# Down stage of a transformer block kernel: operands fetched ahead into idle buffers, fill work finished earlier, products reordered, last product split by bank

## The chip, the cores and the metric

One core of one Trainium2 chip. The metric is the device time of one execution in microseconds (us). A profile is of one execution and gives its span, from the first to the last instruction, which is some 2 us shorter than the device time. The engines are TensorE (PE in the profile; PEld is its weight load), VectorE (DVE), ScalarE (ACT) and SyncE, whose queue (SPq) issues nearly all transfers. PSUM is the memory that TensorE writes its results to; a tile in it is an accumulator, and a bank is a part of it. To evict an accumulator is to read its result out on another engine; a snap is such a read that adds an earlier sum, so that TensorE may go on in the same accumulator.

## The reference

The reference is one transformer block on 2048 tokens of width 1024: a linear-attention half, then a gated MLP half.

```python
h  = x + A_ref(layernorm(x), wqkv, wo)          # attention half, not touched by the change
# MLP half, on layernorm(h)
gate = x @ W_gate; up = x @ W_up                # 1024 -> 3584
hh   = relu(gate) * up
h2   = h + hh @ W_down                          # 3584 -> 1024
```

The change is about the last line, the down projection, and about what is done for it during gate and up.

## The kernel before

Every large product is computed with Winograd's form of Strassen's scheme: seven block products instead of eight, paid for with sums of blocks on VectorE. In the down stage this is done twice. There are seven *outer* products, of half-size blocks. Products 1 and 7 are then plain matmuls; products 2, 6, 5, 3 and 4 are again split into seven *inner* products, m1 to m7. Outer operand sums are made during the gate/up stage and stored to DRAM; inner operand sums are made on VectorE (t1 to t4 from W_down, s1 to s4 from x) while the outer product ahead is running.

During gate/up the sums of W_down are spread over the windows as *fill* work. There is one buffer, `wraw`, for the raw chunk:

```python
def wd_sums(c):
    def load():   # spool: raw = tile(tag="wraw", bufs=1); two dma_start of 512 KB
    def one():    # t1 = b12 - b11 on VectorE, first reader of raw
    ...           # two, three; four also stores the sums to DRAM
    return [load, one, two, three, four]

# per window (12 us of TensorE), how many fill items:
want = len(fill) // (nwin - k) if nwin - k > 1 else len(fill)
want = min(len(fill), max(want, 0))
```

An outer product that is split into inner ones, with its in-order instruction streams (the order in the program is the order on TensorE and on VectorE):

```python
cur["m1"]()                      # TensorE -> PSUM accumulator A
if prv: prv["11"](); pop()       # pop(): one operand sum of the NEXT product, on VectorE
cur["s1"]()                      # VectorE: snap = A + base
cur["m2"]()
if prv: prv["m4"]()              # rest of the previous product
cur["00"](); pop()               # eviction of an output block
if prv: prv["10"](); prv["m3"]()
late_w()                         # request W of the next product, queue its eight sums
pop()
cur["m6"]()                      # needs s2, t2
if prv: prv["01"]()
pop()
cur["m5"]()                      # needs s1, t1
cur["s2"]()                      # VectorE: second snap of A
pop(2)
cur["m7"]()                      # may overwrite A only after the second snap
```

Its x operand tiles and W tiles come from rotating pools that are opened after the gate/up pools are closed. (cut: attention half, gate/up products, launch; in the block above, the other loads and the third snap)

Of the kernel before, what the change touches and what calls it, by code (L numbers as in the profile page):

```python
# [31 lines left out]
def block_kernel(ctx: ExitStack, tc: tile.TileContext, x, wqkv, wo, wg, wu, wd, out, H: int):  # L32
# [417 lines left out]

    new_hn(0)
    wpool = mctx.enter_context(tc.tile_pool(name="wpool", bufs=2))
# [3 lines left out]
    def load_group(g):  # L456

        tiles, loads = [], []
        for nm, v in (("wg", wg_v), ("wu", wu_v)):
            w_sb = wpool.tile([P, KC, 2, GP * P], BF16, tag=nm, name=nm)  # L460
# [143 lines left out]
    def wd_sums(c):  # L604
# [4 lines left out]
        def load():  # L609
            st["raw"] = raw = spool[0].tile([P, 2, 2, D], BF16, tag="wraw", bufs=1, name="wraw")  # L610
            for k in range(2):
                nc.sync.dma_start(out=raw[:, k], in_=wd_k[:, k, 2 * c:2 * c + 2, :])
            st["b"] = [[raw[:, k, :, j * DW:(j + 1) * DW] for j in range(2)] for k in range(2)]

        def one():
            st["t"] = spool[0].tile([P, 4, 2, DW], FP16, tag="wt", bufs=1, name="wt")
# [104 lines left out]
    prepool = ctx.enter_context(tc.tile_pool(name="prepool", side="right", **reuse))  # L721
# [61 lines left out]

    runs = [(early[f // GP], f, f % GP, [1]) for f in range(NE)]
# [25 lines left out]
    for r, (wt, f, fi, toks) in enumerate(runs):  # L810
        w = [ops() for _, ops in now]
        later = []
        for n, s in enumerate(toks):
# [8 lines left out]
            if r >= NE:  # L822
                want = len(fill) // (nwin - k) if nwin - k > 1 else len(fill)
                want = min(len(fill), max(want, 0))
# [41 lines left out]
            if k == nwin - 1:  # L866
                b11 = [prepool.tile([P, FQ, DW], BF16, tag="b11", name="b11")]
                nc.sync.dma_start(out=b11[0][:], in_=wd_v[:, 0:FQ, 0:DW])
    assert not fill

    HW = DW // 2
    raws = {1: (0, 0), 2: (1, 0), 3: (1, 1)}
    sums_of = {4: 3, 5: 0, 6: 1, 7: 2}
    xslot = {2: H12, 3: S4, 4: H22, 5: S1, 6: S2, 7: S3}
    OUTER = (1, 2, 6, 5, 7, 3, 4)
    INNER = (2, 6, 5, 3, 4)
    outs = {2: (0, 0), 7: (1, 1), 3: (0, 1), 4: (1, 0)}
    full = slice(0, DW)
    ALL = slice(0, NT)

    def plain_mm(ps, x, w, p, kh):
        s, t0 = divmod(2 * p, NT)
        for t in range(2):
            for f in range(FQ):
                nc.tensor.matmul(ps[:, t * NW:(t + 1) * NW], lhsT=x[s][kh][:, f, (t0 + t) * P:(t0 + t + 1) * P],  # L885
                                 rhs=w[kh][:, f, :], start=(kh == 0 and f == 0),
                                 stop=(kh == 1 and f == FQ - 1), skip_group_check=True)

    first_ps = [acc("A")]
    wfirst = [b11[0][:], None]  # L890
    xfirst = [[t[:] for t in row] for row in x1]
    plain_mm(first_ps[0], xfirst, wfirst, 0, 0)
# [13 lines left out]
    def load_half(op, x):  # L906

        k = op["k"]
        w = dpool.tile([P, FQ, DW], BF16, tag="w", bufs=4, name="w")
        if k in raws:  # L910
            i, j = raws[k]
            nc.sync.dma_start(out=w[:], in_=wd_v[:, i * FH + x * FQ:i * FH + (x + 1) * FQ, j * DW:(j + 1) * DW])
        else:
            nc.sync.dma_start(out=w[:].bitcast(FP16), in_=t_dram[sums_of[k]][:, x * FQ:(x + 1) * FQ, :])
        op["wt"][x] = w
        op["w"][x] = w[:] if k in raws else w[:].bitcast(FP16)

    def load_x(op, s, kh):

        k = op["k"]  # L920
        t = (x1pool if op["n"] % 2 == 0 else dpool).tile([P, FQ, SW], BF16, tag="x", bufs=4, name="x")
        nc.sync.dma_start(out=t[:], in_=x_dram[s][kh][:, xslot[k], :, :])
        op["xt"][s][kh] = t
        op["x"][s][kh] = t[:].bitcast(FP16) if k in (3, 5, 6, 7) else t[:]

    def new_op(n):
        return {"n": n, "k": OUTER[n], "wt": [None] * 2, "w": [None] * 2,
                "xt": [[None] * 2 for _ in range(2)], "x": [[None] * 2 for _ in range(2)], "s": {}, "t": {}}
# [157 lines left out]
    for p in range(4):  # L1086
        plain_mm(pss[p], op["x"], op["w"], p, 1)
        sink1(p, pss[p])
        if p >= 1:
            pop(2)  # L1090
# [138 lines left out]
```

## Time and profile before

The median is 764.73 us (three runs, 763.38 to 764.73).

| what | before |
|---|---|
| span | 761.0 us |
| TensorE busy | 721.2 us, 95% |
| TensorE idle or at half clock in the down stage | 11.6 us |
| after the last matmul | 5.4 us |

The page of the kernel before, busy time per engine:

```profile
PE 721.2 (95%) x3951; PEld 381.3 (50%) x4004; DVE 565.7 (74%) x1022; ACT 326.5 (43%) x597; POOL 6.1 (1%) x44
```

The timeline of TensorE before, down stage, only the rows with an idle time. Columns: start us, length us, engine, source line, operation, out<-in, form, number of instructions, and in brackets the idle time before and who ended it.

```profile
602.48 6.20 PE L885 MATMUL accA<-w,x 128*128 128x512 bf16 x28 [3.03 <-DMA w<-in_B_W_down_dram]
...
615.00 3.23 PE L1042 MATMUL accA<-w,x 128*128 128x256 bf16 x28 [0.27 <-DMA x<-x_dram]
...
625.12 4.56 PE L1042 MATMUL accA<-ws,xs 128*128 128x256 f16 x28 [3.83 <-DVE snap L1048]
...
654.33 6.27 PE L1042 MATMUL accA<-w,x 128*128 128x256 f16 x56 [0.20 <-DVE snap L1048]
...
713.38 3.22 PE L1042 MATMUL accY<-w,x 128*128 128x256 bf16 x28 [1.09 <-DMA out_dram<-o]
...
717.40 3.22 PE L1042 MATMUL accA<-ws,xs 128*128 128x256 f16 x28 [0.80 <-DVE snap L1048]
...
724.17 6.27 PE L1042 MATMUL accA<-w,x 128*128 128x256 f16 x56 [0.51 <-DVE snap L1048]
...
752.37 3.22 PE L1042 MATMUL accX<-w,xs 128*128 128x256 f16 x28 [0.52 <-DVE o L1007]
```

Idle before these rows sums to 10.25 us. The row at 625.12 also takes 4.56 us for 28 matmuls where the other rows of 28 of this size take 3.22. The windows view of the kernel before shows why. Columns: window, its length, busy time (and instructions) of PE, PEld, DVE, ACT, POOL, granted TensorE clock, mean busy share of the 16 DMA engines (it can pass 1), GB/s.

```profile
621.00:624.00 3.00, 0.29 (x3) 0.10 (x2) 3.00 (x3) 0.00 (x0) 0.00 (x0) 1.00 1.02 421
625.00:627.00 2.00, 1.88 (x10) 1.28 (x10) 1.88 (x3) 0.00 (x0) 0.00 (x0) 0.50 0.97 401
628.00:630.00 2.00, 2.00 (x21) 1.80 (x19) 1.18 (x2) 0.00 (x0) 0.00 (x0) 1.00 0.98 401
```

In the middle row the clock is 0.50: TensorE runs at half speed after the idle time. In the first row VectorE is busy all the time (3.00 of 3.00 us): it makes the sums that it could not begin earlier. The last two columns show that the DMA engines were full meanwhile (401 to 421 GB/s). What VectorE had waited for in the same stage (view of waits, columns: total, times, longest):

```profile
DVE ws L960 <- DMA w<-in_B_W_down_dram: 11.1, 1, 11.1
DVE xs L973 <- DMA x<-x_dram: 7.4, 3, 6.0
```

It could not make product 2's inner sums until W_down and x had come, and TensorE then waited for VectorE.

### The profile page before, as it was taken

Reading aid. Unit: us, or ns where it says so; the run is one execution under the profiler, and the core shown is the slowest. Engines: PE = TensorE matmul, PEld = TensorE weight load, DVE = VectorE, ACT = ScalarE, POOL = GpSimd, SP = SyncE. Lnnn points to the kernel's source line nnn. Section 1 sums busy time; section 2 is a strip of 40 time slices with the busy share of each in tenths; the row PEclk is TensorE's granted clock in tenths of the full one; section 3 lists DMA queues with packets and bytes.
Section 4 is the critical chain, followed back from the end, with each engine's and each line's share of the span. In section 5 each row is a group of like instructions: output and inputs, shape, how many; then the busy total and the mean of one; then the engine's idle time right before and its main releaser. Section 6 shows DMA issues by size and latency. Waiting matters only on the chain.

```text
span 761.0 us, 10554 instructions
## 1 busy us (share of the span) xinstructions
PE 721.2 (95%) x3951; PEld 381.3 (50%) x4004; DVE 565.7 (74%) x1022; ACT 326.5 (43%) x597; POOL 6.1 (1%) x44
## 2 busy tenths in 40 slices
PE   5999999999889989999999999999999879999996
PEld 2443555444344434444444444444444358875685
DVE  5997654787896767687777877788776279947995
ACT  4876553878768554444444444444434010000000
POOL 0000000000000000000000000000000000000000
PEclk9999999999999999999999999999999999999999
DMA  9665002079767544166438356495543899967713
GB/s 318 153 138 152 1 1 107 5 165 224 193 160 183 121 118 145 42 180 185 147 105 246 102 157 221 165 279 178 177 172 122 292 405 333 362 236 255 266 29 97
DMA packets 146419, 132.03 MB, mean 173 GB/s; under 512 B 50880, under 2 KB 127936, under 8 KB 146368
## 3 DMA queue, kind: packets, MB, share of 16 engines
q1 hardware_dynamic: 138928, 127.16, 55.3%
q10 hardware_dynamic: 7440, 4.20, 1.9%
q8 instruction: 31, 0.51, 0.3%
q14 instruction: 20, 0.16, 0.1%
HBM read 79.95 MB, written 39.85 MB: 157 GB/s over the span
## 4 chain that ended last, share of the span: by engine, by line
PE 65%; DVE 16%; DMA 9%; ACT 5%; issue 2%; SPq 1%; POOL 0%; DVEq 0%; ACTq 0%
PE accA L753 22%; PE accX L753 8%; PE accY L753 8%; DMA x<-x_dram 5%; PE accA L1042 4%; PE attn L517 4%; PE Aq L285 3%; PE Aq L419 2%; PE Eq L285 2%; PE Aq L673 2%; PE accX L1042 2%; PE accY L1042 2%; DVE stats L254 2%; DVE o L1007 1%; DMA hn<-hn 1%
## 5 line engine op out<-in xcount | busy, mean ns | idle before, releaser
L763 ACT ACTIVATE gu<-gu 128x512 bf16<-128x512 bf16 x72 | 45.4, 631 | 122.3 <-DVE gu L762 122.3
L758 ACT COPY snap<-accA 128x1024 f32<-128x1024 f32 x72 | 72.7, 1010 | 44.9 <-PE accA L753 44.8
L517 PE MATMUL attn<-wo_mem,oT 128*128 128x512 bf16 x247 | 57.3, 379 | 4.1 <-DVE o_sb L497 3.4
L753 PEld LDWEIGHTS <-tg 128*128 128x128 f16 x384 | 37.6, 98 | 45.3
L753 PEld LDWEIGHTS <-tu 128*128 128x128 f16 x384 | 37.6, 98 | 45.3
L1042 PEld LDWEIGHTS <-x 128*128 128x128 f16 (+1 forms) x560 | 54.6, 98 | 9.9 <-DMA out_dram<-o 1.3
L152 ACT COPY u<-Aq 128x512 f32<-128x512 f32 x56 | 32.2, 581 | 44.9 <-PE Aq L285 21.3
L762 DVE TENSOR_TENSOR gu<-accY,snap 128x1024 bf16<-128x1024 f32 x36 | 43.9, 1220 | 10.2 <-ACT snap L758 10.2
L753 PE MATMUL accA<-hn,tg 128*128 128x512 f16 (+1 forms) x192 | 49.3, 379 | 0.0
L753 PE MATMUL accA<-hn,tu 128*128 128x512 f16 (+1 forms) x192 | 49.3, 379 | 0.0
L762 DVE TENSOR_TENSOR gu<-accX,snap 128x1024 bf16<-128x1024 f32 x36 | 43.9, 1220 | 7.0 <-ACT snap L758 3.9
L1042 PEld LDWEIGHTS <-xs 128*128 128x128 f16 x420 | 41.7, 99 | 11.1 <-issue 5.7
L753 PEld LDWEIGHTS <-wg 128*128 128x128 bf16 x288 | 28.2, 98 | 34.0
L753 PEld LDWEIGHTS <-wu 128*128 128x128 bf16 x288 | 28.2, 98 | 34.0
L517 PEld LDWEIGHTS <-oT 128*128 128x128 bf16 x256 | 24.9, 97 | 34.9 <-issue 6.7
L885 PEld LDWEIGHTS <-x 128*128 128x128 bf16 (+1 forms) x224 | 21.9, 98 | 29.2 <-issue 3.3
L1042 PE MATMUL accA<-w,x 128*128 128x256 f16 (+1 forms) x280 | 31.7, 273 | 1.0 <-DVE snap L1048 0.7
L766 DVE TENSOR_TENSOR hq<-gu 128x512 bf16<-128x512 bf16 x48 | 20.3, 423 | 14.9 <-ACT gu L763 14.9
L285 PEld LDWEIGHTS <-xT 128*128 128x128 bf16 (+1 forms) x192 | 18.6, 98 | 24.9 <-issue 3.4
L497 DVE TENSOR_TENSOR o_sb<-nd,rd 128x384 bf16<-128x384 f32 (+1 forms) x48 | 22.8, 507 | 8.6 <-ACT rd L496 8.3
L1048 DVE TENSOR_TENSOR snap<-accA,u 128x1024 f32<-128x1024 f32 x16 | 19.4, 1219 | 11.5 <-PE accA L1042 11.5
L519 DVE SCALAR_TENSOR_TENSOR x_res<-attn,x_res 128x512 bf16<-128x512 f32 x32 | 22.0, 688 | 6.3 <-PE attn L517 6.2
(199 smaller groups left out, 1368.4 us busy)
## 6 DMA issues: line engine op xcount, KB each, us to landing
x<-x_dram SPq DMA_DIRECT2D x24, 896.0 KB, 7.2
x_dram<-hq SPq DMA_DIRECT2D x28, 512.0 KB, 3.1
wg<-in_B_W_gate_dram SPq DMA_DIRECT2D x14, 512.0 KB, 5.0
wu<-in_B_W_up_dram SPq DMA_DIRECT2D x14, 512.0 KB, 7.2
wraw<-in_B_W_down_dram SPq DMA_DIRECT2D x14, 512.0 KB, 4.9
x_dram<-hq SPq DMA_DIRECT2D x28, 256.0 KB, 3.0
t_dram<-wt SPq DMA_DIRECT2D x28, 256.0 KB, 2.2
w<-t_dram SPq DMA_DIRECT2D x8, 896.0 KB, 8.4
```

Source lines behind the costliest of these rows:

```text
L152: nc.scalar.copy(out=snaps[nm, v], in_=A[v][:])
L285: nc.tensor.matmul(ps[:], lhsT=left[m - 1][:, kc, r + v * P:r + (v + 1) * P], rhs=right[m - 1][:, kc, :], start=(start and kc == 0), stop= ...
L497: nc.vector.tensor_tensor(out=ov[:, c0:c0 + n], in0=ndv[:, :, 0:P].rearrange("p k (h e) -> p k h e", h=HPC), in1=rd[:, 0:n, :].unsqueeze(3 ...
L517: nc.tensor.matmul(ps[:], lhsT=st["oT"][:, c, :], rhs=wo_sb[:, c, j * NW:(j + 1) * NW], start=(c == 0), stop=(c == KC - 1))
L519: nc.vector.scalar_tensor_tensor(out=h_sb[:, j * NW:(j + 1) * NW], in0=ps[:], scalar=1.0, in1=h_sb[:, j * NW:(j + 1) * NW], op0=ALU.mult, ...
L753: nc.tensor.matmul(ps[:, v, :], lhsT=w[v][n - 1][:, kc, :], rhs=left[n - 1][:, kc, :], start=(t is not None and kc == 0), stop=(kc == KH - ...
L758: nc.scalar.copy(out=st[nm][:], in_=halves(st["A"]))
L762: add(out=g[:], in0=halves(st[nm]), in1=st[base][:], op=ALU.add)
L763: nc.scalar.activation(out=g[:, 0, :], in_=g[:, 0, :], func=ACT.Relu)
L766: add(out=out[q], in0=st[q][:, 0, :], in1=st[q][:, 1, :], op=ALU.mult)
L885: nc.tensor.matmul(ps[:, t * NW:(t + 1) * NW], lhsT=x[s][kh][:, f, (t0 + t) * P:(t0 + t + 1) * P], rhs=w[kh][:, f, :], start=(kh == 0 and ...
L1042: nc.tensor.matmul(pv[:, tt, :], lhsT=left(m)[:, f, tt * P:(tt + 1) * P], rhs=right(m)[:, f, :], start=(t is not None and f == 0 and tt % ...
```

## The change

The intent is to remove these waits. (1) The first operands of the down stage are fetched into buffers of the gate/up stage that fall idle: W_down of product 1 into weight buffers of gate/up, two x operands of product 2 into the buffers `wraw` and `wt` of the fill work, which is done two windows earlier for it. (2) The outer order becomes 1-2-6-5-3-7-4, so that the product before last needs no sums. (3) Operand tiles become two fixed sets used in turn. (4) The last product is drained by bank. The diff cut to its core:

```diff
-                want = len(fill) // (nwin - k) if nwin - k > 1 else len(fill)
-                want = min(len(fill), max(want, 0))
+                want = -(-len(fill) // max(nwin - 2 - k, 1))
 ...
-            if k == nwin - 1:
-                b11 = [prepool.tile(...)]; nc.sync.dma_start(out=b11[0][:], in_=wd_v[...])
+            if k == nwin - 3:
+                for x in range(2):
+                    t = wpools[1].tile(..., tag=("wg", "wu")[x], name="wd")   # idle gate/up weight buffer
+                    wtiles[x] = t[...]; load_w(0, x)
 ...
+    for i, nm in ((1, "wraw"), (0, "wt")):          # idle fill buffers take x of product 2
+        xtiles[1, i, 0] = fpool.tile(..., tag=nm, name="xd")[...]; load_x(1, i, 0)
 ...
-    OUTER = (1, 2, 6, 5, 7, 3, 4)
+    OUTER = (1, 2, 6, 5, 3, 7, 4)
 ...
+    load_x(1, 1, 1, slice(0, FQ - 1))
+    load_x(1, 1, 1, slice(FQ - 1, FQ))              # this row needs the very last store
+    load_w(1, 0); load_w(1, 1); load_x(1, 0, 1)
 ...
+    load_w(2, 1); load_x(2, 1, 1); load_x(2, 0, 1)
+    queue_sums(ops[2])                              # sums of product 6 queued before product 2 starts
 ...
             if tail:
                 cur["snap"]("u3", 1, 1)
-                cur["snap"]("u3f", 1, 0)
                 cur["m4f"]()
                 cur["11"]()
-                cur["m3"]()
+                cur["snap"]("u3f", 1, 0)
+                cur["m3a"]()                        # first bank
                 cur["10f"]()
                 cur["01a"]()                        # evicts the first bank (residual added before)
+                cur["m3b"]()                        # second bank
                 cur["01b"]()
```

(cut: tile bookkeeping, `wraw`/`wt` moved to a pool of their own, residual added to the snap)

More of the change, by code (lines that the diff above doesn't have):

```diff
@@ L449, in new_hn @@
         hns.append([aops.tile([P, KH, SW], FP16, name=f"hs{s}{k}") for k in range(3)])
+    wpools = [None, ctx.enter_context(tc.tile_pool(name="wpool1", bufs=1))]
     new_hn(0)
-    wpool = mctx.enter_context(tc.tile_pool(name="wpool", bufs=2))
+    wpools[0] = mctx.enter_context(tc.tile_pool(name="wpool0", bufs=1))
     wg_v = wg.rearrange("(kc p) (h f) -> p kc h f", p=P, h=2)
@@ L459, in load_group @@
         for nm, v in (("wg", wg_v), ("wu", wu_v)):
-            w_sb = wpool.tile([P, KC, 2, GP * P], BF16, tag=nm, name=nm)
+            w_sb = wpools[g % 2].tile([P, KC, 2, GP * P], BF16, tag=nm, name=nm)
             for h in range(2):
@@ L609, in load @@
         def load():
-            st["raw"] = raw = spool[0].tile([P, 2, 2, D], BF16, tag="wraw", bufs=1, name="wraw")
+            raw = fpool.tile([P, 4 * D], BF16, tag="wraw", name="wraw")[:].rearrange("p (k c d) -> p k c d", k=2, c=2)
             for k in range(2):
@@ L615, in one @@
         def one():
-            st["t"] = spool[0].tile([P, 4, 2, DW], FP16, tag="wt", bufs=1, name="wt")
+            t = fpool.tile([P, 4 * D], BF16, tag="wt", name="wt")
+            st["t"] = t[:].bitcast(FP16).rearrange("p (k c d) -> p k c d", k=4, c=2)
             (b11, b12), _ = st["b"]
@@ L720, in block_kernel @@
     x1pool = ctx.enter_context(tc.tile_pool(name="x1pool", side="right", **reuse))
-    prepool = ctx.enter_context(tc.tile_pool(name="prepool", side="right", **reuse))
+    fpool = ctx.enter_context(tc.tile_pool(name="fpool", side="right", **reuse))
     sctx = ExitStack()
@@ L782, in quad, with w_tile, load_w, x_tile @@
         }
+    HW = DW // 2
+    raws = {1: (0, 0), 2: (1, 0), 3: (1, 1)}
+    sums_of = {4: 3, 5: 0, 6: 1, 7: 2}
+    xslot = {2: H12, 3: S4, 4: H22, 5: S1, 6: S2, 7: S3}
+    OUTER = (1, 2, 6, 5, 3, 7, 4)
+    INNER = (2, 6, 5, 3, 4)
+    outs = {2: (0, 0), 7: (1, 1), 3: (0, 1), 4: (1, 0)}
+    full = slice(0, DW)
+    ALL = slice(0, NT)
+    wtiles = [None] * 4
+    xtiles = {}
+    def w_tile(n, x):
+        t = wtiles[2 * (n % 2) + x]
+        return t if OUTER[n] in raws else t.bitcast(FP16)
+    def load_w(n, x):
+        k = OUTER[n]
+        if k in raws:
+            i, j = raws[k]
+            nc.sync.dma_start(out=w_tile(n, x), in_=wd_v[:, i * FH + x * FQ:i * FH + (x + 1) * FQ, j * DW:(j + 1) * DW])
+        else:
+            nc.sync.dma_start(out=w_tile(n, x), in_=t_dram[sums_of[k]][:, x * FQ:(x + 1) * FQ, :])
+    def x_tile(n, s, kh):
+        t = xtiles[n % 2, s, kh]
+        return t.bitcast(FP16) if OUTER[n] in (3, 5, 6, 7) else t
+    def load_x(n, s, kh, rows=slice(0, FQ)):
+        nc.sync.dma_start(out=xtiles[n % 2, s, kh][:, rows, :], in_=x_dram[s][kh][:, xslot[OUTER[n]], rows, :])
     runs = [(early[f // GP], f, f % GP, [1]) for f in range(NE)]
@@ L865, in block_kernel, with plain_mm @@
             k += 1
-            if k == nwin - 1:
-                b11 = [prepool.tile([P, FQ, DW], BF16, tag="b11", name="b11")]
-                nc.sync.dma_start(out=b11[0][:], in_=wd_v[:, 0:FQ, 0:DW])
-    assert not fill
-    HW = DW // 2
-    raws = {1: (0, 0), 2: (1, 0), 3: (1, 1)}
-    sums_of = {4: 3, 5: 0, 6: 1, 7: 2}
-    xslot = {2: H12, 3: S4, 4: H22, 5: S1, 6: S2, 7: S3}
-    OUTER = (1, 2, 6, 5, 7, 3, 4)
-    INNER = (2, 6, 5, 3, 4)
-    outs = {2: (0, 0), 7: (1, 1), 3: (0, 1), 4: (1, 0)}
-    full = slice(0, DW)
-    ALL = slice(0, NT)
-    def plain_mm(ps, x, w, p, kh):
+            if k == nwin - 3:
+                for x in range(2):
+                    t = wpools[1].tile([P, KC * 2 * GP * P], BF16, tag=("wg", "wu")[x], name="wd")
+                    wtiles[x] = t[:, 0:FQ * DW].rearrange("p (f d) -> p f d", f=FQ)
+                    load_w(0, x)
+    assert not fill
+    def plain_mm(ps, n, p, kh):
         s, t0 = divmod(2 * p, NT)
@@ L884, in plain_mm @@
             for f in range(FQ):
-                nc.tensor.matmul(ps[:, t * NW:(t + 1) * NW], lhsT=x[s][kh][:, f, (t0 + t) * P:(t0 + t + 1) * P],
-                                 rhs=w[kh][:, f, :], start=(kh == 0 and f == 0),
+                nc.tensor.matmul(ps[:, t * NW:(t + 1) * NW], lhsT=x_tile(n, s, kh)[:, f, (t0 + t) * P:(t0 + t + 1) * P],
+                                 rhs=w_tile(n, kh)[:, f, :], start=(kh == 0 and f == 0),
                                  stop=(kh == 1 and f == FQ - 1), skip_group_check=True)
+    for i in range(NS):
+        for kh in range(2):
+            xtiles[0, i, kh] = x1[i][kh][:]
+    for i, nm in ((1, "wraw"), (0, "wt")):
+        t = fpool.tile([P, 4 * D], BF16, tag=nm, name="xd")
+        xtiles[1, i, 0] = t[:, 0:FQ * SW].rearrange("p (f t) -> p f t", f=FQ)
+        load_x(1, i, 0)
     first_ps = [acc("A")]
-    wfirst = [b11[0][:], None]
-    xfirst = [[t[:] for t in row] for row in x1]
-    plain_mm(first_ps[0], xfirst, wfirst, 0, 0)
+    plain_mm(first_ps[0], 0, 0, 0)
     prv["g3"]()
@@ L904, in block_kernel @@
     dpool = ctx.enter_context(tc.tile_pool(name="dpool", **reuse))
-    def load_half(op, x):
-        k = op["k"]
-        w = dpool.tile([P, FQ, DW], BF16, tag="w", bufs=4, name="w")
-        if k in raws:
-            i, j = raws[k]
-            nc.sync.dma_start(out=w[:], in_=wd_v[:, i * FH + x * FQ:i * FH + (x + 1) * FQ, j * DW:(j + 1) * DW])
-        else:
-            nc.sync.dma_start(out=w[:].bitcast(FP16), in_=t_dram[sums_of[k]][:, x * FQ:(x + 1) * FQ, :])
-        op["wt"][x] = w
-        op["w"][x] = w[:] if k in raws else w[:].bitcast(FP16)
-    def load_x(op, s, kh):
-        k = op["k"]
-        t = (x1pool if op["n"] % 2 == 0 else dpool).tile([P, FQ, SW], BF16, tag="x", bufs=4, name="x")
-        nc.sync.dma_start(out=t[:], in_=x_dram[s][kh][:, xslot[k], :, :])
-        op["xt"][s][kh] = t
-        op["x"][s][kh] = t[:].bitcast(FP16) if k in (3, 5, 6, 7) else t[:]
+    for x in range(2):
+        wtiles[2 + x] = dpool.tile([P, FQ, DW], BF16, tag=f"w{x}", name="w")[:]
+        xtiles[1, 1 - x, 1] = dpool.tile([P, FQ, SW], BF16, tag=f"x{x}", name="x")[:]
     def new_op(n):
-        return {"n": n, "k": OUTER[n], "wt": [None] * 2, "w": [None] * 2,
-                "xt": [[None] * 2 for _ in range(2)], "x": [[None] * 2 for _ in range(2)], "s": {}, "t": {}}
+        return {"n": n, "k": OUTER[n], "s": {}, "t": {}}
     queue = []
@@ L946, in a @@
         def a(i, j):
-            return op["x"][i][j]
+            return x_tile(op["n"], i, j)
         def b(i, j):
-            return op["w"][i][:, :, j * HW:(j + 1) * HW]
+            return w_tile(op["n"], i)[:, :, j * HW:(j + 1) * HW]
         def new_s(nm):
@@ L965, in t3 @@
         def t3():
-            T["t3"] = op["wt"][0][:].bitcast(FP16)[:, :, HW:DW]
+            T["t3"] = wtiles[2 * (op["n"] % 2)].bitcast(FP16)[:, :, HW:DW]
             tt(out=T["t3"], in0=b(1, 1), in1=b(0, 1), op=ALU.subtract)
@@ L978, in s3 @@
         def s3():
-            S["s3"] = op["xt"][1][0][:].bitcast(FP16)
+            S["s3"] = xtiles[op["n"] % 2, 1, 0].bitcast(FP16)
             tt(out=S["s3"], in0=a(0, 0), in1=a(1, 0), op=ALU.subtract)
@@ L1000, in load_h, with put @@
             hres[k, s] = v
-    def put(k, s, ts, cs, ps, m):
+    def put(k, s, ts, cs, ps, m, with_h=True):
         i, j = outs[k]
-        o = dpool.tile([P, NT * HW], BF16, tag="o", bufs=3, name="o")
+        o = dpool.tile([P, NT * HW], BF16, tag="o", bufs=4, name="o")
         ov = o[:, 0:(ts.stop - ts.start) * (cs.stop - cs.start)].rearrange("p (t d) -> p t d", t=ts.stop - ts.start)
         add(out=ov, in0=ps, in1=m, op=ALU.add)
-        add(out=ov, in0=ov, in1=hres[k, s][:, ts, cs], op=ALU.add)
+        if with_h:
+            add(out=ov, in0=ov, in1=hres[k, s][:, ts, cs], op=ALU.add)
         t0 = (i * HS + s * SW) // P
@@ L1023, in left @@
         def left(m):
-            return {1: op["x"][0][0], 2: op["x"][0][1], 3: op["s"].get("s4"), 4: op["x"][1][1],
+            return {1: x_tile(op["n"], 0, 0), 2: x_tile(op["n"], 0, 1), 3: op["s"].get("s4"), 4: x_tile(op["n"], 1, 1),
                     5: op["s"].get("s1"), 6: op["s"].get("s2"), 7: op["s"].get("s3")}[m]
         def right(m):
-            w = op["w"]
+            w = [w_tile(op["n"], x) for x in range(2)]
             return {1: w[0][:, :, cols(0)], 2: w[1][:, :, cols(0)], 3: w[1][:, :, cols(1)], 4: op["t"].get("t4"),
@@ L1033, in view, with mm @@
             return st[nm][:].rearrange("p (t d) -> p t d", t=NT)
-        def mm(m, nm, t=None):
+        def mm(m, nm, t=None, ts=range(NT)):
             need(op, *{3: ("s4",), 4: ("t4",), 5: ("s1", "t1"), 6: ("s2", "t2"), 7: ("s3", "t3")}.get(m, ()))
@@ L1039, in mm @@
             pv = view(nm)
-            for tt in range(NT):
+            for tt in ts:
                 for f in range(FQ):
@@ L1048, in snap, with add_h, sink @@
             add(out=st[nm][:], in0=view("A"), in1=base[s][:, :, cols(j)], op=ALU.add)
-        def sink(s, j, nm, m, ts=ALL):
+        def add_h(m, s, j):
+            add(out=st[m][:], in0=st[m][:], in1=hres[k, s][:, :, cols(j)], op=ALU.add)
+        def sink(s, j, nm, m, ts=ALL, with_h=True):
             m = base[s][:, ts, cols(j)] if m is None else st[m][:, ts]
@@ L1054, in sink @@
             else:
-                put(k, s, ts, cols(j), view(nm)[:, ts], m)
+                put(k, s, ts, cols(j), view(nm)[:, ts], m, with_h)
         return {
@@ L1063, in inner @@
             "m4f": lambda: mm(4, "F", "A"), "10f": lambda: sink(1, 0, "F", "u3f"), "snap": snap,
-            "01a": lambda: sink(0, 1, "E", "u2", slice(0, 2)), "01b": lambda: sink(0, 1, "E", "u2", slice(2, 4)),
-            "m7f": lambda: snap("u3f", 1, 0),
+            "01a": lambda: sink(0, 1, "E", "u2", slice(0, 2), False),
+            "01b": lambda: sink(0, 1, "E", "u2", slice(2, 4), False), "h01": lambda: add_h("u2", 0, 1),
+            "m3a": lambda: mm(3, "E", None, (0, 1)), "m3b": lambda: mm(3, "E", None, (2, 3)),
         }
     ops = [new_op(n) for n in range(len(OUTER))]
-    op = ops[0]
-    op["w"][0], op["x"] = b11[0][:], xfirst
-    load_half(op, 1)
-    for n in range(1, 2):
-        load_half(ops[n], 0)
-        load_half(ops[n], 1)
-        for s, kh in ((1, 0), (1, 1), (0, 0), (0, 1)):
-            load_x(ops[n], s, kh)
+    load_x(1, 1, 1, slice(0, FQ - 1))
+    load_x(1, 1, 1, slice(FQ - 1, FQ))
+    load_w(1, 0)
+    load_w(1, 1)
+    load_x(1, 0, 1)
     queue_sums(ops[1])
@@ L1084, in block_kernel @@
     for p in range(1, 4):
-        plain_mm(pss[p], op["x"], op["w"], p, 0)
-    for p in range(4):
-        plain_mm(pss[p], op["x"], op["w"], p, 1)
-        sink1(p, pss[p])
-        if p >= 1:
-            pop(2)
+        plain_mm(pss[p], 0, p, 0)
     load_h(OUTER[1], 0)
     load_h(OUTER[1], 1)
-    pop(8)
+    load_w(2, 0)
+    load_x(2, 0, 0)
+    load_x(2, 1, 0)
+    pop(2)
+    for p in range(4):
+        plain_mm(pss[p], 0, p, 1)
+        sink1(p, pss[p])
+        pop(2)
+    load_w(2, 1)
+    load_x(2, 1, 1)
+    load_x(2, 0, 1)
+    queue_sums(ops[2])
     prv = None
@@ L1101, in early_loads @@
         def early_loads():
+            if nxt and n > 1:
+                load_w(n + 1, 0)
+                for s, kh in ((1, 0), (0, 0), (0, 1)):
+                    load_x(n + 1, s, kh)
             if nxt:
-                load_half(nxt, 0)
-                for s, kh in ((1, 0), (0, 0), (0, 1)):
-                    load_x(nxt, s, kh)
                 load_h(nxt["k"], 0)
         def late_x():
-            if nxt:
-                load_x(nxt, 1, 1)
+            if nxt and n > 1:
+                load_x(n + 1, 1, 1)
         def late_w():
-            if nxt:
-                load_half(nxt, 1)
+            if nxt and n > 1:
+                load_w(n + 1, 1)
                 if nxt["k"] in INNER:
@@ L1144, in block_kernel @@
             cur["s2"]()
+            if tail:
+                cur["h01"]()
             pop(2)
@@ L1163, in block_kernel @@
                 ps = acc(("A", "A", "XY"[n % 2], "XY"[(n + 1) % 2])[p])
-                plain_mm(ps, op["x"], op["w"], p, 0)
-                plain_mm(ps, op["x"], op["w"], p, 1)
+                plain_mm(ps, n, p, 0)
+                plain_mm(ps, n, p, 1)
                 if p == 0 and prv:
```

## The prediction

> **What bounds the kernel now.** TensorE: busy 721.2 of 761.0 us (busy table). In the gate/up stage (420 to 584.8 us) it is busy 164.06 of 164.8 us while VectorE has 129.3, so nothing is to be had. The change leaves the matmuls alone; what it can remove is idle TensorE time in the down stage (from about 590 us) (timeline, waits of TensorE):
> - 3.03 us at 602.5: second half of W_down's first block (DMA, issued at 594.5, when the gate/up pools close).
> - 0.27 us at 615.0 (x).
> - 3.83 us at 625.1, put down to the snap on VectorE. VectorE had waited 11.05 us for W_down and 5.96 us for x and did its eight operand sums (11.7 us) late. Behind it the clock is 0.5 for about 3.4 us, and those 28 matmuls take 4.56 instead of 3.22 us: 1.34 us more. The Trainium skill, "TensorE: Matmul & The Clock Gate" (Part 1), says an idle window of about 3.4 us halves the clock; this trace agrees.
> - 0.20 at 654.3; 1.09 + 0.80 at 713 to 717 and 0.51 at 724 (VectorE: sums against evictions); 0.52 at 752.4.
> Sum 11.6 us. After the last matmul (755.6) come two half evictions with residual add (2.2 us) and 3.2 us of output DMA.
>
> **Why the first gap exists.** From 602.5 to 615 DMA moves 395 GB/s at share 1.04: saturated. Seven 0.92 MB operands and the residuals (7.5 MB, about 19 us) start at 594.5.
>
> **What the change does.**
> 1. Both W_down halves of product 1 arrive during gate/up: the 3.03 us go.
> 2. Two x operands of product 2 arrive before 590; four are left, 3.7 MB, about 9 us, landing near 605. Product 2's sums then end near 613, before it starts (near 611.7). The 0.27, 3.83 and 1.34 us go.
> 3. New: product 6's sums are queued before product 2 begins, so three of them (t1, s1, s2: 4.9 us) precede product 2's second snap instead of two. I expect a new wait of 2 us (1 to 3.5) before product 2's m7.
> 4. Order 3-7-4: product 7 needs no sums, so VectorE is lighter in product 3, but in 7 it carries 3's outputs (0.63 us more on its busy path), 7's evictions and 4's sums. The boundary wait, 1.9 us (7 to 3), becomes about 2.5 (7 to 4). The 0.51 at 724 goes.
> 5. Tail: residual added beforehand, snap split, m3 by bank: the 0.52 us goes, and about 1.1 us after the last matmul.
> 6. Fill work ends two windows earlier (three items a window, 0.7 us each): VectorE has 2.5 us to spare per 12 us window; no cost expected, at most 1 us.
>
> **Sum.** Removed 11.6 + 1.1, left or new 2 + 2.5 + 1.3 (small waits): gain about 6.9 us. All on the critical path, but only 0.9%.
>
> **Predicted 757.8 us, 8 in 10 between 753.5 and 762.5.** Faster by over 2%: 0.03; within 2%: 0.95; slower by over 2%: 0.02.
>
> **What would show it.** Right: no TensorE wait over 1 us between 590 and 615, no 0.5 clock near 625; TensorE idle before product 2's m7 (snap); 2 to 3 us at the 7-to-4 boundary; about 1.5 us of VectorE after the last matmul.
> Wrong: a TensorE wait in gate/up from the denser fill; SyncE held behind the split x load that needs the last store, delaying product 2's weights; SyncE held behind residual loads, delaying product 4's sums.

## More of the kernel before

The accumulator of m3 in the last product is one PSUM tile of two banks.

## The result

The changed kernel takes 771.45 us (median of four runs, 770.92 to 772.02) against 764.06 for the kernel before in the same rounds. The ratio is 1.0103, with a 95% interval of 1.0077 to 1.0129. The change made the kernel about 1% slower, where 0.9% faster was predicted; the time lies outside the predicted range. A later, independent set of five rounds with the same file gave 769.45 against 761.94, ratio 1.0091 (1.0072 to 1.0111).

The page of the changed kernel, to be held against the same line above:

```profile
PE 728.7 (95%) x4004; PEld 382.8 (50%) x4004; DVE 567.8 (74%) x1021; ACT 325.8 (42%) x597; POOL 5.8 (1%) x44
```

TensorE is busy for the same share of a longer span. (The 53 matmul records that the first page lacks are missing records, not work: both have 4004 weight loads.) The timeline of TensorE in the changed kernel, rows with idle time, first in gate/up and then in the down stage:

```profile
464.86 1.02 PE L755 MATMUL accY<-hs,tg 128*128 128x512 f16 x4 [2.93 <-DVE gu L764]
...
466.96 1.02 PE L755 MATMUL accA<-hn,tg 128*128 128x512 f16 x4 [0.22 <-ACT snap L760]
```

```profile
624.33 3.22 PE L1056 MATMUL accA<-ws,xs 128*128 128x256 f16 x28 [0.87 <-DVE snap L1062]
...
633.38 4.88 PE L1056 MATMUL accA<-w,xd 128*128 128x256 f16 x28 [2.78 <-DVE snap L1062]
...
657.27 3.22 PE L1056 MATMUL accA<-wd,x 128*128 128x256 f16 x28 [0.67 <-DVE snap L1062]
...
681.10 4.88 PE L1056 MATMUL accA<-w,xd 128*128 128x256 f16 x28 [2.26 <-DVE snap L1062]
...
742.45 3.22 PE L1056 MATMUL accX<-wd,x 128*128 128x256 f16 x28 [1.73 <-DVE u L1203]
...
746.43 3.22 PE L1056 MATMUL accA<-ws,xs 128*128 128x256 f16 x28 [0.76 <-DVE snap L1062]
...
762.83 2.39 PE L1056 MATMUL accX<-wd,xs 128*128 128x256 f16 x14 [2.49 <-DVE o L1020]
```

The waits that the change was aimed at are gone: nothing at the start of the second half of product 1 (3.03 us before), 0.87 us in place of 3.83 at product 2's m6. But there are new ones. Two of the rows take 4.88 us, another two half-clock windows. This is the account, in the profiled executions, in us:

| where | before | after |
|---|---|---|
| before gate/up: lag from near 80 us (see below: chance) | 0 | 2.3 |
| gate/up, near 465 us | 0 | 2.93 + 0.22 |
| product 1: second half of W_down, x | 3.03 + 0.27 | 0 |
| product 2, m6 | 3.83, and 1.34 at half clock | 0.87 |
| product 2, m7 | 0 | 2.78, and 1.66 at half clock |
| product 6, m7 | 0.20 | 0.67 |
| product 5, m7 | 0 | 2.26, and 1.66 at half clock |
| end of product 7 and the next | 1.09 + 0.80 + 0.51 | 1.73 + 0.76 |
| last product | 0.52 | 2.49, and 0.70 at half clock |
| after the last matmul | 5.4 | 4.0 |
| sum | 17.0 | 25.0 |

The difference of the sums is 8.0 us; the spans differ by 8.2 (769.2 and 761.0). A half-clock cost is the length of the row minus the usual one, as 4.88 - 3.22.

Three of the new waits can be read down to their cause. **In gate/up**, the changed kernel, all engines (SPq rows are the issue of a transfer):

```profile
452.19 3.23 SPq L466 DMA_DIRECT2D wu<-in_B_W_up_dram  x2
...
455.47 2.56 SPq L613 DMA_DIRECT2D wraw<-in_B_W_down_dram  x2
...
462.64 0.69 DVE L620 TENSOR_TENSOR wt<-wraw 128x1024 f16<-128x1024 bf16 x1 [6.03 <-DMA wraw<-in_B_W_down_dram]
...
463.59 1.22 DVE L764 TENSOR_TENSOR gu<-accY,snap 128x1024 bf16<-128x1024 f32 x1
...
464.86 1.02 PE L755 MATMUL accY<-hs,tg 128*128 128x512 f16 x4 [2.93 <-DVE gu L764]
```

At 452 to 455 us two loads of gate/up weights are issued, directly behind them at 455.47 the two halves of a W_down chunk. The first difference of that chunk stands next on VectorE and waits 6.03 us for it. VectorE works strictly in order, so the eviction at 463.59 (line 764), which has nothing to do with W_down, comes late, and TensorE waits 2.93 us for its accumulator. The Trainium skill, "TensorE: Matmul & The Clock Gate" (section on the array's architectural detail, engine queue depths), says that ScalarE and VectorE are strict FIFO; this trace agrees. Here the first reader could start 7.2 us after the issue of its chunk; the chunks issued at 429.99 and 474.63, without a weight load just ahead, were read 5.5 and 5.7 us after issue with no wait.

**Before product 2's m7**, VectorE and TensorE of the changed kernel:

```profile
624.33 3.22 PE L1056 MATMUL accA<-ws,xs 128*128 128x256 f16 x28 [0.87 <-DVE snap L1062]
...
626.25 1.08 DVE L973 TENSOR_TENSOR ws<-wd 128x1792 f16<-128x1792 f16 x1
...
628.05 2.03 DVE L986 TENSOR_TENSOR xs<-x 128x3584 f16<-128x3584 f16 x1 [0.72 <-DMA x<-x_dram]
...
630.17 2.03 DVE L989 TENSOR_TENSOR xs<-xs,x 128x3584 f16<-128x3584 f16 x1
632.11 1.22 DVE L1062 TENSOR_TENSOR snap<-accA,u 128x1024 f32<-128x1024 f32 x1
...
633.38 4.88 PE L1056 MATMUL accA<-w,xd 128*128 128x256 f16 x28 [2.78 <-DVE snap L1062]
```

The sums t1, s1, s2 of product 6 (lines 973, 986, 989) stand ahead of product 2's second snap at 632.11. TensorE had finished m6 and m5 at 630.6 and may not overwrite A until that snap is made.

**In the last product**, the changed kernel:

```profile
758.65 1.69 PE L1056 MATMUL accX<-wd,xs 128*128 128x256 f16 x14
...
762.10 0.68 DVE L1020 TENSOR_TENSOR o<-accX,snap 128x512 bf16<-128x512 f32 x1
762.83 2.39 PE L1056 MATMUL accX<-wd,xs 128*128 128x256 f16 x14 [2.49 <-DVE o L1020]
...
765.26 0.69 DVE L1020 TENSOR_TENSOR o<-accX,snap 128x512 bf16<-128x512 f32 x1 [2.48 <-PE accX L1056]
```

The second half of m3 (762.83) waits 2.49 us for the eviction of the first half (762.10 to 762.78), though that eviction reads the other bank. In the compiled program the first matmul of the second half carries a wait on VectorE, for just this eviction.

### The profile page after: what moved, and what is told of

The parts are those of the page before. It is cut to its first block, busy times and chain, and to the rows that moved or that the text cites. A ratio compares the mean times of both kernels' runs of the same rounds, so it can differ in the third digit from the quotient of the medians.

```text
span 769.2 us, 10616 instructions
## 1 busy us (share of the span) xinstructions
PE 728.7 (95%) x4004; PEld 382.8 (50%) x4004; DVE 567.8 (74%) x1021; ACT 325.8 (42%) x597; POOL 5.8 (1%) x44
## 5 line engine op out<-in xcount | busy, mean ns | idle before, releaser
L1056 PEld LDWEIGHTS <-x 128*128 128x128 f16 (+1 forms) x448 | 43.8, 98 | 8.3 <-issue 2.8
L768 DVE TENSOR_TENSOR hq<-gu 128x512 bf16<-128x512 bf16 x48 | 20.3, 423 | 15.1 <-ACT gu L765 15.1
L1062 DVE TENSOR_TENSOR snap<-accA,u 128x1024 f32<-128x1024 f32 x16 | 19.5, 1220 | 11.7 <-PE accA L1056 11.6
L910 PEld LDWEIGHTS <-x 128*128 128x128 bf16 (+1 forms) x168 | 16.5, 98 | 19.8
L198 ACT ACTIVATE e<-pq_mem,negb 128x512 bf16<-128x512 bf16 x32 | 22.5, 717 | 5.7 <-DVE pq_mem L193 5.2
```

What stands on the lines that cost most here:

```text
L198: nc.scalar.activation(out=e, in_=dst, func=ACT.Exp, bias=negb[:, 0:1], scale=1.0)
L768: add(out=out[q], in0=st[q][:, 0, :], in1=st[q][:, 1, :], op=ALU.mult)
L1056: nc.tensor.matmul(pv[:, tt, :], lhsT=left(m)[:, f, tt * P:(tt + 1) * P], rhs=right(m)[:, f, :], start=(t is not None and f == 0 and tt % ...
L1062: add(out=st[nm][:], in0=view("A"), in1=base[s][:, :, cols(j)], op=ALU.add)
```

## The experiments

All are one file each, correct against the reference, with five rounds against the kernel before on the same chip. The runs with the same time of the kernel before were made together; the three sets ran on three chips, so across sets the ratios are compared, and medians only roughly. "After" is the changed kernel: 771.45 us, ratio 1.0103, in the run of the result.

| run | edit | median us | before, same rounds | ratio to before (95%) |
|---|---|---|---|---|
| e1_fill | after, old fill rule | 765.79 | 764.27 | 1.0026 (1.0007 to 1.0046) |
| e2_tail | after, m3b ahead of the eviction | 769.05 | 764.27 | 1.0074 (1.0050 to 1.0099) |
| e3_snap | after, second snap ahead of third sum | 761.19 | 764.27 | 0.9977 (0.9953 to 1.0001) |
| e5_split | after, split load moved | 769.45 | 764.27 | 1.0073 (1.0051 to 1.0095) |
| e4_order | after, old outer order | 765.63 | 763.11 | 1.0047 (1.0010 to 1.0083) |
| e6_three | after, e1 + e2 + e3 | 754.89 | 763.11 | 0.9893 (0.9868 to 0.9918) |
| e8_four | e6 and fewer sums in product 7 | 753.56 | 763.11 | 0.9873 (0.9851 to 0.9895) |
| b1_fill | before, new fill rule | 766.34 | 763.11 | 1.0043 (1.0020 to 1.0066) |
| b2_fixes | before, the reorderings alone | 761.81 | 761.94 | 0.9995 (0.9979 to 1.0011) |
| e9_order | e8 with the old outer order | 755.07 | 761.94 | 0.9910 (0.9891 to 0.9928) |
| a2_again | after, unaltered | 769.45 | 761.94 | 1.0091 (1.0072 to 1.0111) |

### e1_fill and b1_fill: the fill rule

```diff
 e1_fill (on after)
-                want = -(-len(fill) // max(nwin - 2 - k, 1))
+                want = len(fill) // (nwin - k) if nwin - k > 1 else len(fill)
+                want = min(len(fill), max(want, 0))
 b1_fill (on before): the reverse
```

> The changed kernel with only the old rule for the fill work (two or three items per window, ending in the last window). Theory: in the changed kernel the load of a W_down chunk and the first difference that reads it (single buffer) fall so close together, behind a gate/up weight load, that VectorE sits 6.0 us on it and TensorE 2.93 + 0.22 us at 464 to 467 us. With the old rule that wait goes, about 3.1 us less: 768.3 us, no TensorE wait over 0.5 us between 440 and 590. Rival: the wait comes from the weight buffers being in other places or from chance in the transfers; then it stays, about 771.4. In both cases the waits of the down stage stay as they are (0.9, 2.8, 0.7, 2.3, 1.7, 0.8, 2.5 us).

> The kernel before with only the new fill rule (three items per window, done two windows early). Theory: the wait on the W_down chunk behind the gate/up weight load is made by the fill rule alone, so it must appear here too: a TensorE wait of about 3 us near 460 to 467 and 3 us more than before: 767.4. Rival: it needs the weight buffers' new places; then 764.3.

With the old rule no wait of TensorE is left between 440 and 585 us, and from there on the execution runs 3.5 us earlier against the changed kernel than just before it; the ratio fell by 0.0077, some 5.9 us, more than expected. The excess is not settled: 1.0 us of it is, in the profiled executions, already there at 212 us, where the instructions of both are the same and in the same order, and the waits of the down stage are the same ones (0.40, 3.17, 1.06, 2.09, 1.72, 0.76, 2.49); behind the 3.17 us, though, the 28 matmuls took 6.03 us, at half clock for 6.83 us. One source of the excess: in a2_again (the changed kernel again) the wait in gate/up brought half clock from 462.5 to 469.3 us,

```profile
463.71 1.86 PE L755 MATMUL accY<-hs,tg 128*128 128x512 f16 x4 [3.30 <-DVE gu L764]
465.37 1.91 PE L755 MATMUL accY<-hs,tu 128*128 128x512 f16 x4
```

where such rows take 1.02 us otherwise. That cost some 2.8 us besides the 3.30, and e2_tail shows the like (3.74 us, clock low from 463.6 to 470.5, some 2.5 us more). In the first profile of the changed kernel there is none of it. So the wait costs some 3 or some 6 us; how often which, no run counts. e1_fill also shows that the fill work need not end early for the prefetch: it ends in the last window here, and product 2's m6 waits 0.40 us.

The kernel before with only the new rule got the wait, in the same place and of the same size. Its timeline, VectorE and TensorE:

```profile
461.89 0.69 DVE L618 TENSOR_TENSOR wt<-wraw 128x1024 f16<-128x1024 bf16 x1 [6.11 <-DMA wraw<-in_B_W_down_dram]
...
464.10 1.02 PE L753 MATMUL accY<-hs,tg 128*128 128x512 f16 x4 [3.00 <-DVE gu L762]
```

and it became 3.2 us slower (766.34 against 763.11). So the fill rule alone makes this wait; the places of the buffers have no part in it. Nor is it chance in the transfers: all seven profiles with the new rule have it (2.93 to 3.74 us), and none of the six with the old one. The rival falls.

### e2_tail: the split by bank

```diff
                 cur["m3a"]()
+                cur["m3b"]()
                 cur["10f"]()
                 cur["01a"]()
-                cur["m3b"]()
                 cur["01b"]()
```

> The changed kernel with the second half of the last product's m3 issued before the eviction of the first half (program order m3a, m3b, 10, 01a, 01b). Theory: m3b waits 2.49 us for the eviction of the other bank because the two halves are one PSUM tile and the wait is set per tile; without it TensorE ends about 2.5 us earlier, and the program too: about 769.0 us. Rival: the evictions on VectorE are the bound at the end and only start when they did; then under 0.5 us.

The wait before the second half is gone from the profile; all 28 matmuls of m3 stand in one row without an idle time:

```profile
762.18 3.22 PE L1056 MATMUL accX<-wd,xs 128*128 128x256 f16 x28
```

From the start of m3 to the end of the last eviction this takes 2.5 us less. The median is 769.05, as expected, but the unaltered kernel had 769.45 in its second set; by the ratios (1.0074 against 1.0103 and 1.0091 in the two sets of the unaltered kernel) the gain is 1.3 to 2.2 us, with intervals that overlap. So it is the profile that shows the gain, not the time. The rival falls: VectorE's evictions came earlier too. The second half writes other addresses than the eviction reads, and the compiled program had a wait between them that is not there in the new order. So the wait was put there by the program, as a guard over the whole tile; that it was the tile, and not something else, that the guard went by is inferred from this. The Trainium skill, "PSUM — Partial Sum Buffer" (summary of rules for kernel authors), advises to read PSUM from a different bank while a matmul runs, and to guard by bank with semaphores. This kernel had the different bank, but a guard per tile. No run here let the eviction of one bank of this tile overlap with matmuls into its other bank, so that overlap itself is not shown.

### e3_snap: the second snap behind the sums

```diff
             if prv:
                 prv["01"]()
-            pop()
             if nxt:
                 load_h(nxt["k"], 1)
             cur["m5"]()
             cur["s2"]()
             if tail:
                 cur["h01"]()
-            pop(2)
+            pop(3)
             cur["m7"]()
```

> The changed kernel with the second snap of every inner product placed before the third of the next product's operand sums, not behind it. Theory: the waits of TensorE before m7 (2.78, 0.67 and 2.26 us, at 633, 657 and 681) are the snap standing behind a sum that waits for its x operand on the in-order VectorE, and two of them are followed by a half-clock window that costs 1.66 us. With the move: about 0.9 us left at the first, none at the others, no half clock there: about 7 us less, 764.4. Rival: the sums are only put off, and the next product's m6 or m5 waits for them instead: under 2 us gained.

The time is 761.19 us. In the profiled execution the waits before m7 are 0.86 us in product 2 and none in 6 and 5, no half-clock window is left in the down stage, and the execution gains 8.7 us on the changed kernel between 605 and 690 us (it is 1.3 us ahead before that, from stages where nothing differs, and 10.1 after). The waits and half-clock stretches of the two timelines account for 8.4 of it. The timeline of TensorE:

```profile
622.77 3.22 PE L1056 MATMUL accA<-ws,xs 128*128 128x256 f16 x28 [0.64 <-DVE snap L1062]
...
629.91 3.22 PE L1056 MATMUL accA<-w,xd 128*128 128x256 f16 x28 [0.86 <-DVE snap L1062]
...
732.38 3.22 PE L1056 MATMUL accX<-wd,x 128*128 128x256 f16 x28 [1.72 <-DVE u L1202]
```

Between 629.91 and 732.38 TensorE is never idle. The sums that were put off are not waited for, so the rival falls here. (It isn't ruled out for good: in e6_three a sum waited 2.48 us for its x operand, and product 6's m4, behind the sums put off, waited 1.15 us.) This is the largest single cause. Moving one line made the changed kernel no slower than the one before.

### e4_order: the order of the products

```diff
-    OUTER = (1, 2, 6, 5, 3, 7, 4)
+    OUTER = (1, 2, 6, 5, 7, 3, 4)
```

> The changed kernel with the old order of the outer products (1-2-6-5-7-3-4) and nothing else. Theory: product 5 is the one whose slot now must hold the next product's sums (product 3's) while their x operand still arrives; with product 7 next there are no sums in it, so the 2.26 us wait before product 5's m7 (681 us) and its half-clock window (1.66 us) go; at product 7's end about 1.9 us stand for 2.49, and 0.5 comes back in product 3: about 4 us less than the changed kernel, 767.5. The 2.78 us in product 2 stays. Rival: the wait before m7 belongs to the position of the snap whatever product comes next; then nothing changes, 771.4.

The wait before product 5's m7 and its half clock are gone, and at the end of product 7 there are 1.07 + 0.81 us in place of 1.73 + 0.76. The wait in product 2 stays (3.17 us). So the new order did expose product 5: in the old order the plain product 7 comes next and needs no sums, in the new one product 3's sums stand in product 5 and wait 3.73 us for their x. First the changed kernel, with the second snap of product 5 behind s1; then product 5's m7 in e4_order, without a wait:

```profile
677.88 2.02 DVE L986 TENSOR_TENSOR xs<-x 128x3584 f16<-128x3584 f16 x1 [3.73 <-DMA x<-x_dram]
679.83 1.22 DVE L1062 TENSOR_TENSOR snap<-accA,u 128x1024 f32<-128x1024 f32 x1
...
675.21 3.22 PE L1056 MATMUL accA<-w,xd 128*128 128x256 f16 x28
```

This is one of the waits that e3_snap removes while it keeps the new order, so the two gains are not to be added. The six runs of this kernel range from 762.09 to 771.93, and their mean clock from 0.997 to 0.991, so the 5.8 us between the medians are a rough measure; by the ratios to the two sets of the unaltered kernel it is 3.4 to 4.3 us, near the 4 expected.

### e5_split: the load that needs the last store

```diff
     load_x(1, 1, 1, slice(0, FQ - 1))
-    load_x(1, 1, 1, slice(FQ - 1, FQ))
     load_w(1, 0)
     load_w(1, 1)
+    load_x(1, 1, 1, slice(FQ - 1, FQ))
     load_x(1, 0, 1)
```

> The changed kernel with the last row of product 2's x operand (which needs the very last store) requested after the two W_down halves of product 2 and not before them. Theory: that request holds the SyncE queue 4.2 us, W_down lands at 611.2 and the sums of product 2 end at 623; with the move it lands near 606, the sums end near 618, the 0.87 us wait before m6 goes and the 2.78 before m7 shrinks to about 2: 1.7 us less, 3.3 if the half clock goes too, so 768 to 770. Rival: the transfers are limited by throughput then, and nothing moves: 771.4.

The time, 769.45, is in the expected range, but not for the expected reason. In the profiled execution the first W_down half was there at 607.77 and not 611.18, and then s1 waited for the last row of x until 610.76; the sums ended at 621.7, the waits in products 2, 6 and 5 became 1.25, 2.10, 1.18 and 2.18 us in place of 0.87, 2.78, 0.67 and 2.26, and nothing is gained in the down stage: this execution was 1.8 us ahead before it and 1.6 us at the end. So nothing was won in the down stage: one operand was had earlier for another later. The rival is nearer to the truth. The Trainium skill, "Trainium Kernel Development and Optimization" (key constraints), says that all transfers run on the same 16 DMA engines and interleave; that fits, with a mean busy share of the DMA engines of 0.93 between 598 and 612 us in the changed kernel (windows view). This run also shows that a time alone can agree with a wrong reason: the unaltered kernel had the same median, 769.45, in a2_again.

### e6_three and e8_four: the remedies together

```diff
 e6_three = e1_fill + e2_tail + e3_snap;  e8_four also, in the plain product 7:
                 add(out=u2[s][:, ts, :], in0=v, in1=u2[s][:, ts, :], op=ALU.add)
-                pop(2)
+                if p < 2:
+                    pop(2)
```

> The changed kernel with three edits together: old fill rule, second snap ahead of the third sum, m3b ahead of the first half's eviction. Theory: the waits are at different places and add: from the profile 3.15 (fill) + 8.2 (snap, with two half-clock windows) + 3.0 (tail, with its half clock) = 14.3 us less than 771.45: 757; from the medians of the three single runs 18.4 less: 753. I expect 753 to 758, about 1% faster than the kernel before. Rival: they mask one another, and it stays above 761 (no better than the snap alone).

> The three edits and a fourth: in product 7 only the first four of product 4's sums are made, the other four inside product 4, where VectorE is idle for 5 us. Theory: the 1.72 + 0.76 us at the boundary from 7 to 4 are VectorE's backlog of sums ahead of product 7's last eviction and product 4's first snap; with 5.9 us of sums taken out of it both waits go: 2.0 to 2.5 us less than the three edits. Rival: the sums put off hold up m7 or m4 of product 4, or the tail: no gain.

Both came out as expected: 754.89 and 753.56 us. The causes add: by the ratios to the second set of the unaltered kernel (1.0091), the three edits alone gave 5.0, 1.3 and 8.7 us, and together 15.1. The waits of TensorE in the down stage of e8_four are all that is left of the 11.6 us of before:

```profile
619.36 3.22 PE L1057 MATMUL accA<-ws,xs 128*128 128x256 f16 x28 [0.85 <-DVE snap L1063]
...
626.45 3.22 PE L1057 MATMUL accA<-w,xd 128*128 128x256 f16 x28 [0.82 <-DVE snap L1063]
...
727.41 3.22 PE L1057 MATMUL accX<-wd,x 128*128 128x256 f16 x28 [0.21 <-DVE u L1203]
...
743.32 3.22 PE L1057 MATMUL accX<-wd,xs 128*128 128x256 f16 x28 [0.31 <-DVE o L1021]
```

The e8_four kernel is 1.27% faster than the kernel before and, by the medians of different rounds, 2.3% faster than the changed one. By the medians the fourth edit is worth 1.3 us, under what was expected, and the intervals of the two ratios overlap; in the profile 2.3 us of waits went (1.72 and 0.76 became 0.21 and none) and 0.31 came at the last m3.

### b2_fixes and e9_order: controls

b2_fixes is the kernel before with the edits of e3_snap and of product 7, which need nothing of the change. e9_order is e8_four with the old outer order.

> Control: the kernel before with the two VectorE reorderings of the best version that do not need the change (second snap ahead of the third sum; four of the sums after product 7 put off). Theory: what the best version gains (9.6 us) is mostly the early fetch, 3.03 + about 4.6 us, and the tail; here only the small waits (0.2, 1.1, 0.8, 0.5) can go and 3.03 + 0.27 + 3.83 + 1.34 us stay: about 2 us less than before, 761. Rival: the gain of the best version is the reorderings and the change gives nothing: about 755.

> The best version (four edits) with the old order 1-2-6-5-7-3-4. Theory: with the snap ahead and the sums put off, the new order has nothing left to win or lose but the sums that stand in product 3 again and near the tail: within 1.5 us of the four edits (753.6), rather above. Rival: the new order is what made room at the end, and the old one costs 3 us or more.

b2_fixes gains nothing (0.9995), less even than the 2 us expected: 2.92 us for W_down, with 1.69 us at half clock behind it, and 1.89 before m6 stay, and a wait of 1.53 us for the second snap appears at 744 us, in the last product. So the gain of e8_four needs the change itself, once what the change broke is mended. e9_order, in the same rounds, has the same outer order and the same two reorderings as b2_fixes and is 6.7 us faster (755.07 against 761.81): so much are the early operands, the fixed operand sets and the new tail worth together. No run separates these three. e9_order has a ratio of 0.9910 against 0.9873, about 2.8 us by the ratios and 1.5 by the medians, from different rounds whose intervals just touch; that is a little more than the 1.5 us allowed. In its profile the last product's m7 waits 1.52 us for its second snap (738 us), as it does in b2_fixes; e8_four has no such wait. So the new order is probably worth one to three us at the end, once the snap no longer stands behind a waiting sum.

### a2_again: what comes back

> The changed kernel once more, unaltered, to see which of its waits come back. Theory: 3.2 us in gate/up, 0.9 + 2.8 + 0.7 + 2.3 + 1.7 + 0.8 + 2.5 in the down stage come back within 0.6 us each; the 2.2 us wait at 76 us in the first stage and the half clock at 77 us are chance and differ: time 770 to 772. Rival: the early wait and its half clock belong to the changed kernel and come back as they were.

The seven waits of the down stage came back: 0.52, 3.15, 0.61, 2.17, 1.73, 0.76 and 2.49 us, and 3.30 us in gate/up. The half clock did not come back everywhere: there was none behind the 3.15 us, but there was in gate/up (see e1_fill). The wait near 76 us was 1.36 us (2.25 in the first profile, 1.38 in the kernel before), with no half clock behind it. Up to there the instruction orders of both kernels are the same, and over all thirteen profiles of both families this wait went from 0.49 to 2.33 us. So the 2.3 us of the first stage in the account above are chance in when a weight load lands. The median of the unaltered kernel was 769.45 us, a little below the 770 to 772 expected; relative to the kernel before it is the same as in the first set.

## Why the prediction was wrong, point by point

The waits that were to go did go (steps 1 and 2). What failed is the cost of what the change adds: step 6 (the fill work, "no cost expected, at most 1 us"), step 5 (the tail), the effect of the new order on product 5 (step 4), and the half clock, which was left out of the waits that the prediction did foresee.

- **Removed waits (steps 1 and 2): right.** 3.03, 0.27, 3.83 and 1.34 us were to go; 0.87 was left. Its inner working was off: the sums of product 2 were to end near 613 us and ended at 623.1, or 617.7 when the 5.4 us lag of that execution is taken off, because W_down came at 611.2. The expected hold of SyncE behind the split load was real (4.2 us), but e5_split shows that nothing is won by moving it.
- **Step 3, "a new wait of 2 us (1 to 3.5) before product 2's m7": mechanism right, half clock left out.** The wait was 2.78 and 3.15 us in two profiles, within the range, and 2.78 us brought a half-clock window that cost 1.66 more. The prediction used the half clock to explain the kernel before and did not ask whether the new waits would bring it back.
- **Step 4, the reorder: half right.** The 7-to-4 boundary was to be about 2.5 us and was 1.73 + 0.76 = 2.49. But the step looked only at product 7. It missed that product 3's sums now fall into product 5: 2.26 us and 1.66 at half clock, put in the sum under "1.3 (small waits)". e4_order takes it away.
- **Step 5, the tail: wrong in sign.** "The 0.52 us goes, and about 1.1 us after the last matmul": 1.4 us went after the last matmul, but 2.49 + 0.70 us came before the last half in place of 0.52. The prediction took the split by bank as a split of the dependency. e2_tail shows that it was not.
- **Step 6, "no cost expected, at most 1 us": wrong.** It cost 3.15 us here and 3.2 us alone in b1_fill. The prediction named this wait under "Wrong", so it was thought of, but the step counted VectorE's spare time per window (2.5 us of 12) and not what one in-order instruction does when it waits 6 us for a transfer. The kernel before already showed such a wait in its view of waits, 3.9 us in two cases, at which TensorE did not wait.
- **The sum.** It allowed 2 + 2.5 + 1.3 = 5.8 us for left and new waits. They were 15.6 in the down stage and 3.15 in gate/up: 13 us too few; the other 2.3 us of that profile were chance.

## What to carry to other kernels

On an in-order engine, ask of every instruction that waits for a transfer what stands behind it: an eviction that frees an accumulator should stand ahead of any work that may wait, and here one such move was worth 8.7 us, more than the 7.6 us (8.47 of waits less the 0.87 left) that the prefetch removed. Put distance, not only spare time, between a load and its first reader, and check behind which larger load it is issued. A split by bank helps only if the dependency is split too, so look in the compiled program at what the second half waits for.

## What the Trainium skill lacked or had wrong

- "TensorE: Matmul & The Clock Gate" says that the clock halves after at least one idle window of about 3.4 us and advises against gaps over about 3 us. Here shorter waits did it: 2.78 and 2.26 us in the changed kernel, 2.17 us in a2_again, 2.09 us in e1_fill, while 3.00 us (b1_fill), 3.03 us (before) and 3.15 us (a2_again, product 2) did not. The window's free run, which the page describes, fits this; how much of a window must be idle is not on the page. Worked out from the 13 profiles: within each, the moments at which the clock dropped lie on a grid of 3.41 us. Each of the 27 grid windows before a drop was at least 56% idle, and no other window was more than 55% idle while the clock was full (from 20 us on, up to the last matmul). So 2.26 us that fall into one window (66% idle at 678.33 to 681.74, changed kernel) cost more than 3.15 us cut by a window's edge (49% and 43%, a2_again). Ends of matmuls are modelled in a profile, so the limit is not sharp. What a stretch costs, 1.34 to 1.66 us (28 matmuls in 4.56 to 4.88 us instead of 3.22), agrees with half speed over part or all of 3.4 us; in three places the clock stayed low for a second window, 6.83 us, which cost 2.5 to 2.8 us (e1_fill, e2_tail, a2_again).
- "PSUM — Partial Sum Buffer" advises guarding by bank; it lacks the warning that a tile over two banks may be guarded as one: 2.49 us in each of the profiles that have the split in its first form.
